# Turned rows of X: DRAM writes issued from another queue, and the last batch's staging tiles in another ring

## The chip, the cores and the metric

The kernel runs on one NeuronCore of a Trainium2 chip. The metric is the device time of one execution in microseconds (us). The core has five engines with instruction streams of their own: TensorE (PE in the profile), VectorE (DVE), ScalarE (ACT), GpSimd (POOL) and SyncE (SP). SP does nothing here but issue DMAs; GpSimd computes and can issue DMAs too. Each issuing engine has a DMA queue of its own, and all queues are served by the same 16 DMA engines.

## The reference, cut to what matters

Shapes: batch B = 4, sequence S = 448, model width DM = 768. Three stages follow one another:

```python
x = sigmoid_attention(q, k, v)                 # (4, 448, 768)
u = x + (x.T @ U @ V).T                        # mixing over tokens, low rank
x = u + relu(u @ w_ch1) @ w_ch2                # inner width 3072
theta = x @ w_theta
y = w_tok_r @ (x * cos(theta)) + w_tok_i @ (x * sin(theta))   # mixing over tokens
u = x + y
out = u + relu(u @ w_ch)
```

All is float32; each matrix product is done as three products of a high and a low part.

## The kernel before

X is kept on chip in one tile `X[128, 6, 1792]`: partitions and the index d (0 to 5) hold the 768 columns of the model, the last axis the 4 x 448 tokens. The order of instructions on each engine is the order in which the code issues them; nothing is reordered afterwards.

**The multilayer stage.** `i` runs over 12 slices of the inner width and `b` over the 4 batches. `ch1(i, b)` makes a slice (36 matmuls, L665 to L667), `ch2(i, b)` multiplies it back (three PSUM tiles `y`, numbered e2 = 0 to 2, two buffers; L687 to L689), and VectorE adds each `y` tile to X (L691). `ch2` runs one batch behind `ch1`. After each `y` tile a hook issues side work: steps of weight conversion on VectorE, ScalarE and GpSimd, and, in the last slice (`i == L`), the turns described now.

**The turns.** The last stage needs X with tokens on the partitions. VectorE turns each 128x448 piece of X in blocks of 32x32 (`turn_x`, L717) into a staging tile, and a DMA of 224 KB writes that tile to the DRAM array `x_d` (L718). There are 24 such pieces, six for each batch. Those of batches 0 to 2 are turned in the hooks of the last slice, two after each `y` tile, into the tile `stg` with three buffers: the fourth turn has to wait until the first turn's write has landed, and so on. Those of batch 3 come after the last `ch2`, into buffers of the tags `t1` and `t2` (two buffers each), so that the fifth turn there waits for the first one's write.

**The theta stage.** The 1792 tokens are taken in 14 chunks c of 128. `project(c, ...)` multiplies a chunk by w_theta (six weight rows `th_r`, kk = 0 to 5, L809 to L813) into one of two PSUM buffers `th`. `trig(c)` reads that buffer on VectorE (L845, L846) and makes sine and cosine on ScalarE. `load_xn(c)` reads a chunk of `x_d` with four DMAs (L822), `zmake(c)` multiplies, and `zsplit` splits the products into high and low parts in the rings `zh` and `zl` of 12 buffers each; the low parts are made on GpSimd (L112). `mix(b)` is the mixing over tokens (L909 to L914). The first two chunks are begun before the last two rows of w_theta have come: `project` is called for kk = 0 to 3 of chunks 0 and 1, then for kk = 4 and 5. Rows 4 and 5 of w_theta are loaded (`load_kept`, L236) from DRAM on SP's queue as soon as the last `ch2` has released their buffers. Behind them on SP's queue, in this order, stand the eight reads of `load_xn(0)` and `load_xn(1)`, and then the six writes of batch 3's turns.

Of the kernel before, what the change touches and what calls it, by code (L numbers as in the profile page):

```python
# [11 lines left out]
F32 = mybir.dt.float32  # L12
# [12 lines left out]
def tile_kernel(  # L25
# [15 lines left out]
    nc = tc.nc  # L41
    B, H, S, D = q.shape
# [3 lines left out]
    P = 128  # L46
# [8 lines left out]
    HN = DM // 2  # L55
# [44 lines left out]
    def pool(name, side="left", space=None):  # L100
        st = ExitStack()
        kw = dict(name=name, bufs=1, side=side, reuse_waits="tile")
        if space is not None:
            kw["space"] = space
        return st.enter_context(tc.tile_pool(**kw)), st
# [107 lines left out]
    x_d = dpool.tile([DM, NT], F32, name="x_d")  # L213
# [385 lines left out]
    for p in range(NP):  # L599
# [19 lines left out]
        b, r = divmod(p - 2 - NH, NH)  # L619
# [3 lines left out]
        b, r = divmod(p - 3 - NH, NH)  # L623
# [91 lines left out]
    ps_y, ps_y_st = pool("ps_y", "left", PSUM)  # L715
    def turn_x(b, d, t):
        nc.vector.transpose(out=t, in_=X[:, d, b * S:(b + 1) * S])  # L717
        nc.sync.dma_start(out=x_d[d * P:(d + 1) * P, b * S:(b + 1) * S], in_=t)  # L718

    def hook(i, b):  # L720
        def after(e2):
            if i == L and 0 < b < B:
                for d in (2 * e2, 2 * e2 + 1):
                    turn_x(b - 1, d, late["stg"].tile([P, S], F32, tag="stg", name=f"stg_{b}_{d}", bufs=3))
            if (i, b) == (0, 1):
                ps = ps_g.tile([P, FB, 512], F32, tag="g", name=f"hl_{e2}", bufs=2)
                U2(B - 1, 2 * e2, ps, (vhl, vll))
            if i == 0 and b in (1, 2):
                split_u(b + 1, u23, 2 * e2, 2 * e2 + 2, lo_pool)
            tick(i, b, e2 + 2)  # L730
        return after
# [63 lines left out]
    zp, st = pool("zp")  # L795
# [122 lines left out]
    load_xn(0)  # L918
    load_xn(1)
    for d in range(NK):  # L920
        tag = f"t{d % 2 + 1}"
        t = zp.tile([P, 2, HN], F32, tag=tag, name=f"stg_{B}_{d}", bufs=2).rearrange("p a n -> p (a n)")[:, :S]
        turn_x(B - 1, d, t)
    project(0, th_t, "th", 0, 4)
    project(1, th_t, "th", 0, 4)
# [108 lines left out]
```

## Time and profile before

| | us |
|---|---|
| median of three runs | 1178.91 (1177.11 to 1180.7) |
| the profiled execution, its own time | 1180.31 |
| its span, first to last instruction | 1178.5 |
| PE busy | 1153.6 (98%) |
| DVE busy | 667.1 (57%) |
| ACT busy | 360.3 (31%) |
| POOL busy | 190.9 (16%) |

The multilayer stage's last slice runs from about 820 to 883 us of the span, the theta stage from 883 to 1035. A busy share is an average over the whole span. PE stands still for 25 us in all, so what matters for the time is in which places those lie and what ends each.

### The profile page before, as it was taken

The page shows a single profiled execution, that of the slowest core. Times are in us where ns is not written, and L with a number is a line of the kernel's source. Part 1 is how long each engine was busy: PE and PEld are TensorE (multiplying, and loading weights), DVE is VectorE, ACT ScalarE, POOL GpSimd, SP SyncE. Part 2 cuts the span into 40 slices and gives each one's busy share as a digit, 9 for nine tenths or more (in the row PEclk, how much of TensorE's full clock was granted, in tenths as well). Part 3 has the DMA queues.
Part 4 walks back from the last instruction along what each step waited for, and adds up shares of the span by engine and source line. Part 5 has one row for each costly group of instructions (what it writes and reads, how often), then busy time and mean ns, then how long its engine had stood idle before and what let it go on. Part 6 is the DMA issues. An engine that isn't in the chain of part 4 may idle for free.

```text
span 1178.5 us, 15645 instructions
## 1 busy us (share of the span) xinstructions
PE 1153.6 (98%) x6336; PEld 995.9 (85%) x6336; DVE 667.1 (57%) x829; ACT 360.3 (31%) x465; POOL 190.9 (16%) x138
## 2 busy tenths in 40 slices
PE   7999999999999999999999999999998999999998
PEld 4354458999999999999999999999888899999997
DVE  4777873445555655556555656565485742833443
ACT  5878872221212121212121213131114431630110
POOL 2300012211211021102110212121001421320000
PEclk9999999999999999999999999999998999999999
DMA  9887730113231322132213333332557311230444
GB/s 163 157 175 134 159 83 1 55 54 96 71 111 54 96 84 98 54 96 85 96 54 97 96 107 107 107 108 107 210 204 177 55 22 20 44 145 1 57 65 67
DMA packets 227944, 111.20 MB, mean 94 GB/s; under 512 B 192384, under 2 KB 218880, under 8 KB 227744
## 3 DMA queue, kind: packets, MB, share of 16 engines
q1 hardware_dynamic: 201024, 98.57, 32.2%
q0 software_dynamic: 2368, 8.24, 2.6%
q10 hardware_dynamic: 24480, 3.39, 2.0%
q8 instruction: 50, 0.82, 0.3%
q14 instruction: 22, 0.18, 0.1%
HBM read 86.51 MB, written 23.66 MB: 93 GB/s over the span
## 4 chain that ended last, share of the span: by engine, by line
PE 87%; DVE 5%; DMA 4%; SPq 2%; issue 1%; ACT 1%; POOL 0%; ACTq 0%; DVEq 0%
PE g L665 10%; PE g L666 10%; PE g L667 10%; PE y L687 9%; PE y L689 9%; PE y L688 9%; PE av L420 4%; PE sc L394 3%; PE y L909 3%; PE y L910 3%; PE y L911 3%; PE wc L996 2%; PE wc L998 2%; PE wc L997 2%; DMA q<-in_q_dram 2%; PE th L813 1%
## 5 line engine op out<-in xcount | busy, mean ns | idle before, releaser
L691 DVE TENSOR_TENSOR X<-y,X 128x896 f32<-128x896 f32 x144 | 157.0, 1091 | 112.4 <-PE y L689 111.0
L687 PE MATMUL y<-gh,w 128*128 128x448 f32 x576 | 211.5, 367 | 4.8 <-DVE X L691 4.8
L689 PE MATMUL y<-gh,w 128*128 128x448 f32 x576 | 211.0, 366 | 0.0
L688 PE MATMUL y<-gl,w 128*128 128x448 f32 x576 | 210.9, 366 | 0.0
L665 PE MATMUL g<-uh,w 128*128 128x448 f32 x576 | 210.9, 366 | 0.0
L666 PE MATMUL g<-ul,w 128*128 128x448 f32 x576 | 210.5, 365 | 0.0
L667 PE MATMUL g<-uh,w 128*128 128x448 f32 x576 | 210.4, 365 | 0.0
L672 ACT ACTIVATE gh<-g 128x896 fp32r<-128x896 f32 x48 | 44.1, 919 | 393.0 <-PE g L667 393.0
L673 DVE SCALAR_TENSOR_TENSOR gl<-g,gh 128x896 fp32r<-128x896 f32 x48 | 52.4, 1092 | 174.8 <-ACT gh L672 174.8
L112 POOL TENSOR_TENSOR w<-ca_w,w 128x768 fp32r<-128x768 f32 x42 | 77.8, 1853 | 432.0 <-ACT w L109 432.0
L687 PEld LDWEIGHTS y<-gh,w 128*128 128x128 f32 x576 | 108.5, 188 | 15.8 <-DVE X L691 5.0
L665 PEld LDWEIGHTS g<-uh,w 128*128 128x128 f32 x576 | 108.3, 188 | 9.9 <-ACT uh L109 0.7
L689 PEld LDWEIGHTS y<-gh,w 128*128 128x128 f32 x576 | 108.5, 188 | 8.6
L688 PEld LDWEIGHTS y<-gl,w 128*128 128x128 f32 x576 | 108.5, 188 | 8.5
L667 PEld LDWEIGHTS g<-uh,w 128*128 128x128 f32 x576 | 108.3, 188 | 8.6
L666 PEld LDWEIGHTS g<-ul,w 128*128 128x128 f32 x576 | 108.3, 188 | 8.6
L385 ACT ACTIVATE A<-sc,bias_s 128x896 f32<-128x896 f32 x72 | 72.0, 1006 | 23.1 <-PE sc L394 13.3
L420 PE MATMUL av<-A,v 128*64 128x448 f32 x288 | 64.5, 556 | 0.0
L909 PE MATMUL y<-tok,zh 128*128 128x448 f32 x168 | 61.6, 367 | 1.4 <-DVE X L914 1.4
L809 PE MATMUL th<-th_r,xh 128*128 128x384 f32 x168 | 57.5, 342 | 4.8 <-DVE t L846 4.8
L112 POOL TENSOR_TENSOR zl<-t,zh 128x768 fp32r<-128x768 f32 x23 | 43.6, 1920 | 114.3 <-ACT zh L109 78.0
L911 PE MATMUL y<-tok,zl 128*128 128x448 f32 x168 | 61.5, 366 | 0.0
(142 smaller groups left out, 1645.7 us busy)
## 6 DMA issues: line engine op xcount, KB each, us to landing
ws_w<-in_moe_w_ch_dram SPq DMA_DIRECT2D x40, 768.0 KB, 4.4
ws_w<-in_moe_w_ch_dram POOLq DMA_DIRECT2D x8, 768.0 KB, 6.2
x_d<-stg SPq DMA_DIRECT2D x24, 224.0 KB, 2.0
k<-in_k_dram SPq DMA_DIRECT2D x94, 56.0 KB, 2.5
q<-in_q_dram SPq DMA_DIRECT2D x93, 56.0 KB, 3.4
xn<-x_d SPq DMA_DIRECT2D x52, 96.0 KB, 3.3
ws_th<-in_moe_w_theta_dram SPq DMA_DIRECT2D x6, 768.0 KB, 4.4
th_d<-sp_th SPq DMA_DIRECT2D x6, 768.0 KB, 4.0
```

The costliest lines, as they stand in the source:

```text
L112: nc.gpsimd.tensor_sub(o, a, b)
L385: nc.scalar.activation(a, ps, AF.Sigmoid, bias=bias_s, scale=SCALE)
L420: nc.tensor.matmul(ps[h * D:(h + 1) * D, :S], v_t[p // 2][:, 2 * (p % 2) + h, c, :], A_t[p, c][:, h, :], start=c == 0 and p % 2 == 0, stop ...
L665: nc.tensor.matmul(o, wh[:, sl], uh_t[b][:, kk, :], start=kk == 0, stop=False)
L666: nc.tensor.matmul(o, wh[:, sl], ul_t[b][:, kk, :], start=False, stop=False)
L667: nc.tensor.matmul(o, wl[:, sl], uh_t[b][:, kk, :], start=False, stop=kk == NK - 1)
L687: nc.tensor.matmul(o, wh[:, sl], gh[:, j, :], start=j == 0, stop=False)
L688: nc.tensor.matmul(o, wh[:, sl], gl[:, j, :], start=False, stop=False)
L689: nc.tensor.matmul(o, wl[:, sl], gh[:, j, :], start=False, stop=j == FB - 1)
L691: nc.vector.tensor_add(x, ps[:, :, :S], x)
L909: nc.tensor.matmul(o, zh[:, sl], tok_h[:, i, :], start=n == 0, stop=False)
L911: nc.tensor.matmul(o, zl[:, sl], tok_h[:, i, :], start=False, stop=n == NZ - 1)
```

## The change

All 24 writes of turned pieces are issued by GpSimd in place of SP. The six staging tiles of batch 3 come from the ring `zh` (12 buffers) in place of `t1` and `t2` (two each), so that each of the six has a buffer of its own.

```diff
@@ -715,7 +715,7 @@
     def turn_x(b, d, t):
         nc.vector.transpose(out=t, in_=X[:, d, b * S:(b + 1) * S])
-        nc.sync.dma_start(out=x_d[d * P:(d + 1) * P, b * S:(b + 1) * S], in_=t)
+        nc.gpsimd.dma_start(out=x_d[d * P:(d + 1) * P, b * S:(b + 1) * S], in_=t)
@@ -918,8 +918,7 @@
     load_xn(0)
     load_xn(1)
     for d in range(NK):
-        tag = f"t{d % 2 + 1}"
-        t = zp.tile([P, 2, HN], F32, tag=tag, name=f"stg_{B}_{d}", bufs=2).rearrange("p a n -> p (a n)")[:, :S]
+        t = zp.tile([P, 2, HN], F32, tag="zh", name=f"stg_{B}_{d}", bufs=12).rearrange("p a n -> p (a n)")[:, :S]
         turn_x(B - 1, d, t)
```

## Rows read from the trace of the kernel before

**Rows 1.** Windows: length, busy us of five engines, PEclk, DMA share, GB/s
```profile
834.00:848.00 14.00, 14.00 (x71) 12.97 (x70) 5.35 (x9) 0.92 (x1) 0.00 (x0) 1.00 0.92 365
848.00:856.00 8.00, 5.14 (x24) 4.08 (x23) 7.93 (x11) 2.51 (x3) 0.00 (x0) 0.98 0.24 86
856.00:859.00 3.00, 3.00 (x10) 2.69 (x9) 2.97 (x4) 0.00 (x0) 0.00 (x0) 0.50 0.45 158
859.00:884.00 25.00, 23.04 (x112) 20.42 (x111) 19.95 (x27) 4.04 (x5) 1.85 (x1) 1.00 0.60 224
884.00:896.00 12.00, 12.00 (x70) 11.74 (x68) 2.82 (x5) 0.85 (x1) 0.00 (x0) 1.00 1.01 248
896.00:901.00 5.00, 0.16 (x2) 0.13 (x1) 3.29 (x5) 0.18 (x1) 0.00 (x0) 0.91 0.86 291
901.00:907.00 6.00, 6.00 (x19) 6.00 (x20) 3.87 (x5) 5.89 (x7) 0.00 (x0) 0.51 0.37 57
...
934.00:1035.00 101.00, 100.56 (x542) 96.83 (x543) 53.05 (x61) 40.49 (x49) 28.42 (x17) 1.00 0.24 45
```

**Rows 2.** VectorE's timeline, first stall: start, us, operation, [idle before <- releaser]
```profile
835.65 1.17 DVE L717 STREAM_TRANSPOSE stg<-X 128x448 f32<-128x448 f32 x2
...
847.20 0.65 DVE L717 STREAM_TRANSPOSE stg<-X 128x448 f32<-128x448 f32 x1 [8.25 <-DMA x_d<-stg]
```

**Rows 3.** Tile view of x_d, the write issued at 836.3
```profile
DMA to landing us min/median/max: 10.8/10.8/10.8
```

**Rows 4.** TensorE's timeline, 849 to 855
```profile
849.74 0.47 PE L687 MATMUL y<-gh,w 128*128 128x448 f32 x1 [0.65 <-DVE X L691]
...
854.65 0.47 PE L687 MATMUL y<-gh,w 128*128 128x448 f32 x1 [2.21 <-DVE X L691]
```

**Rows 5.** VectorE's timeline, second stall
```profile
884.60 2.22 DVE L717 STREAM_TRANSPOSE stg<-X 128x448 f32<-128x448 f32 x4
...
897.67 1.19 DVE L717 STREAM_TRANSPOSE stg<-X 128x448 f32<-128x448 f32 x2 [10.85 <-DMA x_d<-stg]
898.80 0.96 DVE L845 TENSOR_SCALAR t<-th 128x768 f32<-128x768 f32 x1
```

**Rows 6.** SP's timeline, 884 to 900 (its own time)
```profile
884.69 9.78 SPq L822 DMA_DIRECT2D xn<-x_d  x8
894.57 4.65 SPq L718 DMA_DIRECT2D x_d<-stg  x6
```

**Rows 7.** Tile view of th_r, the last of the six loads
```profile
L236 SPq DMA_DIRECT2D th_r<-th_d x1: 858/858/858, 883.8 to 883.8; - x1
...
DMA to landing us min/median/max: 8.5/8.5/8.5
```

**Rows 8.** TensorE's timeline around the second stall and after
```profile
891.74 0.33 PE L809 MATMUL th<-th_r,xh 128*128 128x384 f32 x1
...
892.78 0.33 PE L809 MATMUL th<-th_r,xh 128*128 128x384 f32 x1
...
900.90 0.66 PE L809 MATMUL th<-th_r,xh 128*128 128x384 f32 x1 [4.84 <-DVE t L846]
...
933.84 0.47 PE L909 MATMUL y<-tok,zh 128*128 128x448 f32 x1 [1.39 <-DVE X L914]
```

**Rows 9.** Tile view of ws_U, eight loads issued from GpSimd
```profile
L271 POOL DMA_DIRECT2D ws_U<-in_moe_U_dram x8: 546/590/673, 30.5 to 34.5; - x8
...
DMA to landing us min/median/max: 2.2/3.9/6.0
```

**Rows 10.** Windows, as rows 1, during those loads
```profile
32.00:34.00 2.00, 2.00 (x16) 0.42 (x14) 1.93 (x5) 1.97 (x3) 2.00 (x5) 1.00 1.02 191
```

**Rows 11.** VectorE's timeline, last two turns of batch 2
```profile
877.79 1.17 DVE L717 STREAM_TRANSPOSE stg<-X 128x448 f32<-128x448 f32 x2
```

**Rows 12.** Tile view of x_d, the third and fourth writes of batch 2
```profile
L718 SPq DMA_DIRECT2D x_d<-stg x2: 320/320/320, 875.4 to 875.9; - x2
...
DMA to landing us min/median/max: 2.0/2.0/2.0
```

## The prediction

> **What bounds the kernel now.** I read windows over the stages around the turns first, for where PE stands still and at which clock, then the timelines of VectorE, PE and SP at the two places that the windows point to. PE is the bound nearly everywhere: from 934 to 1035 it is busy 100.56 of 101 us [rows 1], so whatever is gained or lost before 934 is carried to the end, and nothing later is touched by the change. The idle time that the change can reach lies at two places, and each begins with VectorE waiting for a write to `x_d`.
>
> First place. At 835.65 VectorE makes the first two turns of batch 0. The fourth must have the first one's buffer back. That write was issued at 836.3 and landed 10.8 us later [rows 3], so VectorE stood still for 8.25 us before 847.20 [rows 2]. The DMA engines were busy 0.92 of the time at 365 GB/s from 834 to 848 [rows 1], with loads that SP had issued ahead of the turns. The reader is to see the cost two steps on: PE needs `y` buffers that the late additions on VectorE release, and stands still for 0.65 us before 849.74 and 2.21 us before 854.65 [rows 4]. Then its granted clock is at 0.50, that is 1.2 GHz, from 856 to 859, and 0.98 as a mean in the 8 us before [rows 1]. That costs 3 x 0.5 + 8 x 0.02 = 1.7 us more. PE's other idle time here, 1.96 us from 859 to 884 [rows 1], falls where VectorE is busy for 19.95 of 25 us with other work; it stays.
>
> Second place. At 884.60 VectorE makes four turns of batch 3 and then waits 10.85 us, until 897.67, for the first write [rows 5]. SP could not issue that write before 894.57, since the eight reads of `x_d` ahead of it took SP from 884.69 to then [rows 6], with the DMA engines busy 1.01 from 884 to 896 [rows 1]. Behind the waiting turn on VectorE stand the last turn and `trig(0)`, which begins at 898.80 [rows 5]. PE, out of PSUM buffers, stands still for 4.84 us until 900.90 [rows 8] and then runs at a clock of 0.51 until 907 [rows 1]. After that PE isn't the bound for a while: at 933.84 it still waits 1.39 us for VectorE's addition [rows 8], so the chain of VectorE that starts with `trig(0)` sets the time there. What counts at this place is by how much `trig(0)` starts earlier; the slow clock from 901 to 907 is absorbed and I count it at nothing.
>
> **The change part by part.** *Removed from SP.* 24 issues of 0.32 us each [rows 12], on an engine that computes nothing: worth nothing by itself. What stood behind them on SP, reads of later chunks, goes out sooner; those aren't late now.
>
> *Added on GpSimd.* Each issue occupies the engine: 0.59 us is the median of eight loads that GpSimd issued around 30 us [rows 9], so 24 x 0.59 = 14 us on an engine that does no work of its own from 834 to 859 and 1.85 us of it from then to 884 [rows 1]. In program order a low part of a converted weight stands behind the last writes of batch 2, and the low parts of the theta stage behind those of batch 3; both are needed after these writes have long been issued. Zero, as long as VectorE's turns aren't late.
>
> *Landing time of a write from GpSimd's queue.* The trace has no write from there. The nearest rows are those eight loads of 16 and 96 KB: 2.2 us at least, 3.9 median, 6.0 at most [rows 9], with the DMA engines busy 1.02 and VectorE 1.93 of 2 us [rows 10]. A write on SP with the DMA engines free lands in 2.0 us [rows 12]. I take 3.9 us, since both places of interest are busy too; 2.0 and 6.0 are the bounds.
>
> *First place after.* The first write lands at 836.3 + 3.9 = 840.2 in place of 847.1, the fourth turn comes 7 us earlier, and so does the addition that PE lacked before 849.74 and 854.65. Gain: 0.65 + 2.21 + 1.7 = 4.5 us. Even at 6.0 us the turn would be 4.8 us earlier, enough for both gaps.
>
> *A new wait.* The three `stg` buffers remain. The tightest place is the sixth turn of a batch, which needs the third one's write: that was issued at 875.4 [rows 12], and the sixth turn begins half of 1.17 us after 877.79 [rows 11], at 878.4. The room is 3.0 us. SP's 2.0 us fits; 3.9 us is late by 0.9 us. Behind that turn on VectorE stand a conversion step and the addition for which the last `ch2` waits. In batches 0 and 1 VectorE has idle time to take it up; in batch 2 I count 0.9 us. Bounds: 0, and at 6.0 us a loss of 3.0. First place together: 4.5 - 0.9 = 3.6 us.
>
> *Second place after.* The six turns of batch 3 wait for nothing: VectorE is through with them some 3.5 us after 884.60. `trig(0)` then waits for PE to finish `project(0)`. In the profile PE began row kk = 4 of chunk 0 at 891.74 and kk = 5 at 892.78 [rows 8], 1.04 us each, so `project(0)` ends at about 893.9. At best `trig(0)` begins there, 898.8 - 893.9 = 4.9 us earlier. But the writes now go out while w_theta's row 5 is still coming. It was issued at 883.8 and landed 8.5 us later, at 892.3 [rows 7], 0.5 us before PE used it, with the DMA engines saturated. Six writes are 6 x 229,376 bytes = 1.38 MB; at 365/0.92 = 397 GB/s [rows 1] that is 3.5 us of all DMA engines. If most of it gets between, say 3.0 us, row 5 lands at 895.3, PE waits 2.5 us for it, `project(0)` ends at 896.4 and `trig(0)` begins at 896.5: 2.3 us gained. If all 3.5 us come first and that row runs at half clock, 0.8 us is gained; if none does, 4.9. I take 2.3, as the writes are all issued within 4 us and well before row 5 would be through. The reads of chunks 0 and 1 are delayed likewise, but their products come some 8 us behind `trig(0)`.
>
> *The rest.* `t1`, `t2` and `zh` keep their sizes; the z tiles that take over the six buffers come more than 10 us after those writes.
>
> **Sum.** 3.6 + 2.3 = 5.9 us. The profiled span becomes 1178.5 - 5.9 = 1172.6, its execution 1180.31 - 5.9 = 1174.4. The median of the runs shown is 1.4 us under that execution, so I predict 1178.91 - 5.9 = 1173.0 us.
>
> **The rivals.**
>
> *Row 5 isn't delayed* (its packets go first, or the writes are slow to start). Then 3.6 + 4.9 = 8.5 us: 1170.4. For it: the load is issued 1 us or more ahead of the first write. Against it: at 1.01 busy, what is put in has to push something out.
>
> *The queue makes no difference at the first place*: the writes still land in some 10 us from 834 to 848, because the same DMA engines are full. Then only the second place gains, 2.3 us: 1176.6. For it: 365 GB/s of loads is in the way whoever issues. Against it: loads from GpSimd landed in 3.9 us with the engines 1.02 busy; but SP's backlog at that moment was perhaps shorter. The Trainium skill, DMA: Bandwidth & Descriptors, section Issuing engines are not separate DMA queues, says that DMAs of all issuing engines run on the same 16 engines and that spreading them saves only issue time; by that rule alone it is this rival. The same page, section Queues, rings and completion order, has each DMA engine taking turns between the queues' rings by packet, which would let a short write pass a long backlog; no run here shows either for a write.
>
> *Slower: GpSimd can't prepare its transfers while VectorE is busy.* VectorE works almost without a gap where the turns stand. If each write then lands L us after issue, the sixth turn of each of three batches is late by L - 3.0. At L = 9 that is 6 us a batch. Batch 0's is less than the present stall of 8.25 us; the other two cost 12 us, of which the 5 us that VectorE idles between 859 and 884 [rows 1] take part. Net 7 lost there, 2.3 won later: 1178.9 + 4.7 = 1183.6. It decides from L of about 7 us. Against it: the eight loads took GpSimd 0.55 to 0.67 us each [rows 9], with VectorE busy 1.93 of 2 us [rows 10]. The Trainium skill, SBUF — State Buffer, section SBUF: two separate sides, says that GpSimd can't write its descriptors while a VectorE operation of a two-port mode runs, and that such a DMA seems blocked; by that rule the time goes towards this rival, and the early loads here don't show such a delay.
>
> *No gain*: another wait of VectorE's chain, such as ScalarE's or GpSimd's low parts, eats the second place, and the new wait the first. 1178 to 1179.
>
> **How the numbers follow.** Chances: forecast 0.48 (own range 1171 to 1175.4), row 5 undelayed 0.20, no difference at the first place 0.17, starved GpSimd 0.10, no gain 0.05. 0.3% of 1178.9 is 3.5 us, about what a measurement can tell. Faster by more, under 1175.4: 0.46 + 0.20 + 0.06 of the third (if row 5 isn't late there either) = 0.72. Within it: 0.02 + 0.11 + 0.05 = 0.18. Slower: 0.10. Range: at best 4.5 + 4.9 = 9.4 gives 1169.5, and a little for the measurement 1168.5; at the upper end it takes in the third case and stops at 1178, leaving out the slower one and part of the last.
>
> **What would show it.** VectorE's wait for a write at the fourth turn of batch 0 under 3 us, and none in batch 3; PE's gaps of 0.65 and 2.21 us gone, with no clock of 0.50 there; a wait of PE for `th_r` of about 2.5 us before kk = 5 of chunk 0; writes landing in 3 to 5 us. I'd be wrong if a write lands in over 7 us, if new waits for `x_d` stand at the sixth turns, or if PE's wait for `th_r` is over 4 us.

## The result, and the profile after

The changed kernel took 1168.4 us (median of five runs, 1167.84 to 1169.27), the kernel before 1178.48 us beside it: ratio 0.9915, 95% interval 0.9901 to 0.993. The gain is 10.1 us where 5.9 was forecast, and 1168.4 lies 0.1 us below the range. A second set of runs of the same kernel (the last experiment) gave 0.9933 (0.9919 to 0.9948), a gain of 8.5 us. The profiled execution shown here took 1167.84 us, with a span of 1166.1.

The first turn of batch 0 stands at 833.58 in this profile and at 835.65 in that of before [rows 2]. What lies ahead of it isn't touched by the change, so these 2.07 us are a difference of two executions, and I take them off below.

Windows of the changed kernel over the same stages as [rows 1], each about 2 us earlier at the first place, columns as there:

```profile
832.00:846.00 14.00, 14.00 (x71) 12.97 (x70) 8.60 (x13) 1.39 (x2) 3.11 (x6) 1.00 0.92 378
846.00:854.00 8.00, 8.00 (x40) 7.22 (x40) 7.90 (x11) 1.82 (x3) 1.44 (x3) 1.00 0.44 162
854.00:857.00 3.00, 3.00 (x17) 2.78 (x16) 2.96 (x5) 0.00 (x0) 1.07 (x2) 1.00 0.87 278
...
886.00:891.00 5.00, 4.82 (x26) 4.18 (x25) 3.27 (x4) 3.42 (x4) 0.00 (x0) 1.00 0.96 236
...
901.00:906.00 5.00, 3.16 (x17) 2.55 (x16) 4.97 (x4) 2.63 (x3) 3.54 (x2) 0.99 0.00 0
906.00:909.00 3.00, 3.00 (x11) 3.00 (x10) 2.97 (x5) 2.43 (x3) 1.81 (x2) 0.50 0.02 5
```

In the second line PE is busy 8.00 of 8 us where it was 5.14, and in the third the granted clock is 1.00 where it was 0.50. Behind the turns of batch 3, where TensorE had 0.16 us of work in 5 us before, the line from 886 to 891 shows 4.82. A stretch at 0.50 (1.2 GHz) is left at 906, behind a stretch in which PE was busy 3.16 of 5 us (901 to 906).

VectorE's timeline of the changed kernel, the lines that answer to [rows 2, 5, 11], with two more that the explanation needs:

```profile
833.58 1.17 DVE L717 STREAM_TRANSPOSE stg<-X 128x448 f32<-128x448 f32 x2
...
841.84 0.65 DVE L717 STREAM_TRANSPOSE stg<-X 128x448 f32<-128x448 f32 x1 [4.96 <-DMA x_d<-stg]
...
870.88 1.30 DVE L717 STREAM_TRANSPOSE stg<-X 128x448 f32<-128x448 f32 x2
...
877.87 3.27 DVE L717 STREAM_TRANSPOSE stg<-X 128x448 f32<-128x448 f32 x6
...
887.70 0.96 DVE L845 TENSOR_SCALAR t<-th 128x768 f32<-128x768 f32 x1 [6.55 <-PE th L813]
...
893.14 0.96 DVE L118 TENSOR_TENSOR xl<-X,xh 128x768 fp32r<-128x768 f32 x1 [0.77 <-ACT xh L109]
```

The fourth turn still waits, but 4.96 us instead of 8.25. The six turns of batch 3 run as one piece. `trig(0)` (L845) now waits for TensorE, not for a turn. The last line is the low part of X for a later chunk; before, VectorE's timeline had it so:

```profile
905.57 0.96 DVE L118 TENSOR_TENSOR xl<-X,xh 128x768 fp32r<-128x768 f32 x1 [2.10 <-ACT xh L109]
```

With three marks the whole difference can be read off, each as a distance between two instructions, so that the 2.07 us drop out:

| stretch on VectorE | before | after | gained |
|---|---|---|---|
| first turn of batch 0 to first turn of batch 3 | 48.95 | 44.29 | 4.66 |
| from there to `trig(0)` | 14.20 | 9.83 | 4.37 |
| from there to that `xl` | 6.77 | 5.44 | 1.33 |
| from there to the end of the span | 272.93 | 272.96 | 0 |

The sum is 10.36 us; the spans differ by 1178.5 - 1166.1 - 2.07 = 10.33. The first two terms are the two places of the forecast (3.6 and 2.3 us there), the third it didn't have.

Some 1.2 to 1.6 us of the first term belong to this one execution of the kernel before. Three kernels below keep the writes of batches 0 to 2 on SP and so have the same stall: the ring alone, batch 3 from GpSimd, and the early sine. Their first stretch is 47.40, 47.70 and 47.42 us. TensorE's two gaps are there (0.48 to 0.76 and 2.21 to 2.22 us), but its granted clock stays at 1.00 behind them, where [rows 1] have 0.50 for 3 us. The kernel with the early sine, its windows and VectorE's timeline:

```profile
847.00:855.00 8.00, 5.12 (x25) 4.09 (x23) 7.93 (x11) 2.51 (x3) 0.00 (x0) 1.00 0.24 86
855.00:858.00 3.00, 3.00 (x16) 2.79 (x15) 2.97 (x4) 0.00 (x0) 0.00 (x0) 1.00 0.45 158
```
```profile
834.67 1.17 DVE L717 STREAM_TRANSPOSE stg<-X 128x448 f32<-128x448 f32 x2
...
882.09 2.21 DVE L717 STREAM_TRANSPOSE stg<-X 128x448 f32<-128x448 f32 x4
```

The kernels that write batches 0 to 2 from GpSimd take 43.99 to 44.46 us for this stretch. Beside the three executions without the slow clock the first place thus gains 2.9 to 3.7 us. In how many executions of the kernel before the clock falls there isn't known. The second term varies as well: the second profile of the changed kernel has 10.31 us in place of 9.83, a gain of 3.89.

The landing times, from the tile views of the changed kernel: the first write of batch 0 (issued at 834.5), and the third and fourth writes of batch 2, which answer to [rows 3, 12]:

```profile
L718 POOL DMA_DIRECT2D x_d<-stg x1: 790/790/790, 834.5 to 834.5; - x1
...
DMA to landing us min/median/max: 7.3/7.3/7.3
```
```profile
L718 POOL DMA_DIRECT2D x_d<-stg x2: 540/540/540, 871.8 to 872.5; - x2
...
DMA to landing us min/median/max: 2.2/2.3/2.3
```

Among the loads a write from GpSimd lands in 7.3 us, where SP's took 10.8; for the later writes of batch 2 it is 2.2 to 2.3, where SP's took 2.0. The last load of w_theta's row 5, answering to [rows 7]:

```profile
L236 SPq DMA_DIRECT2D th_r<-th_d x1: 849/849/849, 876.9 to 876.9; - x1
...
DMA to landing us min/median/max: 9.4/9.4/9.4
```

It is 0.9 us slower than the 8.5 of before, not 3.0. TensorE began kk = 4 at 884.99 and kk = 5 at 886.33, which is 0.3 us more than the 1.04 us that a row takes. In the second profile of this kernel row 5 landed in 9.9 us and kk = 5 began 0.8 us late.

### The profile page after: what moved, and what is told of

Same layout as the page of the kernel before. It is cut to its first block, busy times and chain, and to the rows that moved or that the text cites. A ratio compares the mean times of both kernels' runs of the same rounds, so it can differ in the third digit from the quotient of the medians.

```text
span 1166.1 us, 15652 instructions
## 1 busy us (share of the span) xinstructions
PE 1149.5 (99%) x6336; PEld 993.5 (85%) x6336; DVE 667.5 (57%) x829; ACT 360.1 (31%) x465; POOL 204.2 (18%) x162
## 4 chain that ended last, share of the span: by engine, by line
PE 90%; DVE 3%; SPq 3%; DMA 2%; issue 1%; ACT 0%; POOL 0%; ACTq 0%; DVEq 0%
PE g L665 10%; PE g L667 10%; PE g L666 10%; PE y L687 10%; PE y L689 10%; PE y L688 10%; PE av L420 4%; PE sc L394 3%; PE y L909 3%; PE y L910 3%; PE y L911 3%; PE wc L995 2%; PE wc L996 2%; PE wc L997 2%; PE th L813 2%; SPq L319 1%
## 5 line engine op out<-in xcount | busy, mean ns | idle before, releaser
L909 PE MATMUL y<-tok,zh 128*128 128x448 f32 x168 | 61.6, 367 | 0.0
L910 PE MATMUL y<-tok,zh 128*128 128x448 f32 x168 | 61.5, 366 | 0.0
```

Source lines behind the costliest of these rows:

```text
L909: nc.tensor.matmul(o, zh[:, sl], tok_h[:, i, :], start=n == 0, stop=False)
L910: nc.tensor.matmul(o, zh[:, sl], tok_l[:, i, :], start=False, stop=False)
```

## The experiments

The diffs are against the changed kernel, but for the fifth. Each group ran beside the kernel before on one chip.

### One part at a time: four kernels

**The ring alone.** All writes on SP as before, batch 3 in the ring `zh`.

```diff
-        nc.gpsimd.dma_start(out=x_d[d * P:(d + 1) * P, b * S:(b + 1) * S], in_=t)
+        nc.sync.dma_start(out=x_d[d * P:(d + 1) * P, b * S:(b + 1) * S], in_=t)
```

> All 24 writes on SP's queue as before; only batch 3's staging tiles move to the ring of 12. Theory A (three separate gains: 4.5 us at the first place from GpSimd's queue, 4.4 us at the second place from six turns that need no buffer back, 1.3 us because ScalarE's table load no longer waits for a staging write): the first place stays, the other two gains remain, 5.7 us under the kernel before, about 1172.8; VectorE's wait of 8.25 us at the fourth turn of batch 0 stays, trig(0) starts when project(0) ends. Rival B (the queue is what counts at both places, since on SP a write stands behind eight reads): no gain over 1 us, 1178.

1172.78 us, ratio 0.9951 (0.9939 to 0.9963). VectorE's timeline of this kernel:

```profile
846.59 0.65 DVE L717 STREAM_TRANSPOSE stg<-X 128x448 f32<-128x448 f32 x1 [8.08 <-DMA x_d<-stg]
...
882.62 3.27 DVE L717 STREAM_TRANSPOSE stg<-X 128x448 f32<-128x448 f32 x6
...
892.04 0.96 DVE L845 TENSOR_SCALAR t<-th 128x768 f32<-128x768 f32 x1 [6.15 <-PE th L813]
```

The first stall is that of before. At the second place `trig(0)` comes 9.42 us after the first turn instead of 14.20: 4.78 us gained, which is the forecast's "best" of 4.9. Row 5 landed in 8.5 us. So the six turns' wait was nearly the whole obstacle there.

**GpSimd's queue for batches 0 to 2 alone.** Batch 3 writes from SP, out of `t1` and `t2`, as before.

```diff
+        (nc.sync if b == B - 1 else nc.gpsimd).dma_start(...)
...
-        t = zp.tile(..., tag="zh", ..., bufs=12)...
+        tag = f"t{d % 2 + 1}"
+        t = zp.tile(..., tag=tag, ..., bufs=2)...
```

> The writes of batches 0 to 2 on GpSimd's queue, batch 3's writes and staging tiles as before. Theory A: only the first place gains, 4.5 us: about 1174.0; the wait of 10.9 us at the fifth turn of batch 3 and the table load's wait stay. Rival C (the first place's gain is swallowed later, since VectorE's chain after 885 waits for a DMA that doesn't come earlier): under 2 us, 1177 or more.

1174.41 us, 0.9959 (0.9947 to 0.9971). The first wait is 4.83 us, the second 10.63, as before. The queue gains 4.8 us (0.0041 x 1179; 3.4 to 6.2 by the interval) at the first place by itself. With the ring's 5.8 us (0.0049 x 1179) it makes 10.6; the two add up to what the change gains within the intervals.

**Batch 3 from GpSimd, the others from SP.**

```diff
+        (nc.gpsimd if b == B - 1 else nc.sync).dma_start(...)
```

> The writes of batches 0 to 2 on SP as before; batch 3 as in the changed kernel (GpSimd's queue and the ring of 12). Theory A: 4.4 + 1.3 = 5.7 us under the kernel before, 1172.8, and the same as with SP's queue for batch 3, since a write that nobody waits for may be issued anywhere. Rival D (the writes on GpSimd's queue hold up the last row of w_theta by some 3 us, as I had forecast, and in the changed kernel something else made up for it): 2 to 3 us slower than the ring alone with SP's queue, 1175 to 1176.

1174.0 us, 0.9953 (0.994 to 0.9966), between the two expected times; the ratio can't be told from that of the ring alone. Row 5 landed in 9.8 us and TensorE's waits list

```profile
PE th L809 <- DMA th_r<-th_d: 0.6, 1, 0.6
```

`trig(0)` came 10.32 us after the first turn, 0.9 later than with the ring alone. So the mechanism of the forecast, the writes delaying row 5, exists, with a wait of 0.6 us where 2.5 was forecast.

**All writes from GpSimd, no ring.** Only the tags `t1` and `t2` of before are put back.

> All 24 writes on GpSimd's queue, batch 3's staging tiles in the two tags of two buffers as before. Theory A: the first place gains 4.5 us; at the second the fifth turn waits for the first write, which lands some 7.4 us after its issue, about when project(0) ends, so most of the 4.4 us is gained, but the table load waits for the fourth turn's write again, so 0 to 1.3 of the 1.3 us: 1169 to 1171. Rival E (the ring of 12 is what counts at the second place): only 4.5 us, 1174.

1171.94 us, 0.9935 (0.9923 to 0.9947), a little above what was expected. VectorE still stands for 6.53 us before the fifth turn, nearly all of it inside its wait for TensorE, since `trig(0)` waits 0.25 us more:

```profile
888.57 1.26 DVE L717 STREAM_TRANSPOSE stg<-X 128x448 f32<-128x448 f32 x2 [6.53 <-DMA x_d<-stg]
890.09 0.96 DVE L845 TENSOR_SCALAR t<-th 128x768 f32<-128x768 f32 x1 [0.25 <-PE th L813]
```

That places `trig(0)` at 10.26 us after the first turn, and the `xl` behind it at 6.78 us after that, as before the change. Together 1.8 us of the 3.5 us that this kernel is behind the changed one. Of the rest, its profile has 1.27 us behind the `xl` (274.23 us to the end of the span instead of 272.96). TensorE's granted clock there is 0.69 as a mean from 911 to 918, behind 7 us in which TensorE was busy 3.86; in the changed kernel the mean from 908 to 915 is 0.90, behind 7 us with 5.16 busy. That this slower clock makes the 1.27 us isn't tested. The 6.78 belongs to the third term.

### The third term: ScalarE's table load

ScalarE must load its table for sine once in the theta stage. Its timeline before and after, around that load:

```profile
893.67 0.85 ACT L109 ACTIVATE xh<-X 128x768 fp32r<-128x768 f32 x1 [12.80 <-PE th L810]
900.82 1.28 ACT L847 ACT_TABLE_LOAD   x1 [6.30 <-DVE t L846]
902.12 0.84 ACT L847 ACTIVATE t<-t 128x768 f32<-128x768 f32 x1
```
```profile
887.33 0.85 ACT L109 ACTIVATE xh<-X 128x768 fp32r<-128x768 f32 x1 [13.38 <-PE th L810]
888.20 1.28 ACT L847 ACT_TABLE_LOAD   x1
889.68 0.85 ACT L847 ACTIVATE t<-t 128x768 f32<-128x768 f32 x1 [0.20 <-DVE t L846]
```

Before, the load starts only when VectorE has made the operand of the sine (L846); after, it runs beside VectorE's work. A load needs no operand, so the reason must be in the program. The compiled one, before and after (the number is the instruction's place on its engine):

```
before  354 L847 ACT_TABLE_LOAD [waits DMAHW1_49,DVE_49]
        355 L847 ACTIVATE ...   [waits Pool_49]
after   354 L847 ACT_TABLE_LOAD
        355 L847 ACTIVATE ...   [waits DVE_49]
```

The sine's tile was a staging tile in the kernel before, so it had several things to wait for, one of them a write to `x_d`, and some of these waits stand in front of the load. With the staging tiles in another ring one wait is left, and it stands on the sine itself. The test is the kernel before with a sine of one column that nothing uses, ahead of the theta stage, so that the table is there early:

```diff
     ch2(*prev, hook(NB - 1, B))
+    nc.scalar.activation(warm, half_pi, AF.Sin)
     th_t[4] = load_kept("th4", "w2")
```

> The kernel before with one sine of a single column added on ScalarE after the last product of the multilayer stage, so that the sine table is loaded while ScalarE is idle. Theory A (in the kernel before, the table load of 1.28 us stood on the path because it had inherited the wait for a staging write and for VectorE; in the changed kernel it runs under VectorE's subtraction): about 1.3 us under the kernel before, VectorE's wait for xh of 2.1 us down to 0.8. Rival F (the 1.3 us come from the earlier start of VectorE's chain): no gain, wait for xh still 2.1 us.

1177.8 us beside 1179.1, ratio 0.9989 (0.998 to 0.9998): 1.3 us by the medians, 0.2 to 2.4 by the interval, in line with the third term. The load stands at 878.36 now, and VectorE's wait for `xh` in its waits list is near that of the changed kernel (0.77), not of before (2.10):

```profile
DVE xl L118 <- ACT xh L109: 0.8, 1, 0.8
```

The Trainium skill, ScalarE: Activation LUTs, section What ACT_TABLE_LOAD costs, gives about 1283 ns for a load, which is the 1.28 us here, and a drain of about 1380 ns besides; no such drain shows, as the sine at 902.12 follows the load's end at 902.10, and in the changed kernel the load at 888.20 follows the conversion's end at 888.18.

### The first place: is a wait of 4.96 us still paid for?

**A fourth staging buffer.** `stg` with four buffers in place of three.

```diff
-  ... late["stg"].tile([P, S], F32, tag="stg", name=f"stg_{b}_{d}", bufs=3)
+  ... late["stg"].tile([P, S], F32, tag="stg", name=f"stg_{b}_{d}", bufs=4)
```

> The changed kernel with four buffers of stg in place of three. VectorE's wait of 5.0 us at the fourth turn of batch 0 goes, or moves to the fifth and shrinks by some 3 us. Theory A (that wait is covered: the addition behind it is early enough for TensorE anyway): no gain, within 0.5 us of the changed kernel, 1168.4. Rival G (the wait still costs TensorE time through the additions that follow): 1 to 3 us faster, 1165.5 to 1167.5.

1169.29 us, 0.992 (0.9907 to 0.9933), the changed kernel's time. VectorE's waits list for writes here, and in the changed kernel:

```profile
DVE stg L717 <- DMA x_d<-stg: 3.0, 2, 2.2
```
```profile
DVE stg L717 <- DMA x_d<-stg: 5.0, 1, 5.0
```

Two microseconds of that wait are gone and nothing is gained, so at least these lay under TensorE's own work, which the changed kernel's windows show without a gap from 832 to 854. The profile is that of the slowest of the six executions, 1173.54 us; its excess lies ahead of the turns, the first of which stands at 839.43, and the stretch from there to the first turn of batch 3 takes 44.00 us.

**ScalarE's queue.** All writes issued by ScalarE.

```diff
-        nc.gpsimd.dma_start(out=x_d[...], in_=t)
+        nc.scalar.dma_start(out=x_d[...], in_=t)
```

> The changed kernel with all writes on ScalarE's queue in place of GpSimd's. Theory A (what matters is a queue other than the one with the loads): the writes land at the first place in about 7 us too, against 7.3 from GpSimd and 10.8 from SP, and in 2 us elsewhere; ScalarE waits behind late turns, which costs at most 2 us: 1168 to 1171. Rival H (writes from GpSimd are served in some other way): they land in 10 us again and the first place's gain is lost: 1173.

1176.01 us, 0.9974 (0.9964 to 0.9983), slower than I expected. The first write landed in 8.4 us, so this queue, too, passes SP's backlog in part, but ScalarE's timeline shows another price:

```profile
835.75 12.51 ACTq L718 DMA_DIRECT2D x_d<-stg  x6
848.36 0.92 ACT L672 ACTIVATE gh<-g 128x896 fp32r<-128x896 f32 x1 [15.07 <-DVE stg L717]
```

Six issues take 12.51 us, as each waits until VectorE has turned its piece, and the conversion of `gh` that TensorE needs stands behind them. TensorE's waits for VectorE's additions sum to 6.1 us; in the changed kernel they are 2.1. Its granted clock was 0.69 as a mean from 870 to 880, behind such waits, where the changed kernel has 1.00. GpSimd was a good place since nothing urgent stands behind a waiting write there.

### The second place: who pays for the six writes?

**Batch 3 from SP, batches 0 to 2 from GpSimd.** Here SP's order puts the six writes behind the reads of chunks 0 and 1, so they can't get between row 5 and its landing.

```diff
+        (nc.sync if b == B - 1 else nc.gpsimd).dma_start(...)
```

> GpSimd's queue for batches 0 to 2, SP's queue and the ring of 12 for batch 3. Theory A: the last row of w_theta lands 8.5 us after issue in place of 9.4, so trig(0) starts 0.3 to 0.9 us earlier than in the changed kernel: 1167.5 to 1168.4. Rival I (batch 3 behind the reads on SP makes a later wait for x_d): 1169 or more.

1168.48 us, 0.9909 (0.9897 to 0.9922); row 5 landed in 8.4 us, and `trig(0)` came 9.39 us after the first turn, 0.4 to 0.9 sooner than in the two profiles of the changed kernel. The time is the changed kernel's within the intervals, so which queue carries batch 3 matters by less than these can tell once the ring is there.

**Twice the bytes.** Batch 3's writes carry each staging tile twice (448 KB, into a wider `x_d`; the second copy is never read).

```diff
+        if b == B - 1:
+            nc.gpsimd.dma_start(
+                out=x_d[d * P:(d + 1) * P, b * S:(b + 2) * S].rearrange("p (a s) -> p a s", a=2),
+                in_=t.unsqueeze(1).to_broadcast([P, 2, S]))
+            return
```

> The changed kernel, but each of batch 3's six writes from GpSimd carries its tile twice (448 KB, into a wider x_d whose last part nobody reads), so 2.75 MB in place of 1.38 stand beside the last load of w_theta. Theory S (while GpSimd's queue has work it gets a share of the DMA engines, whatever is behind; what it takes beyond that comes from the reads of x_d that stand behind the load on SP's queue): the load of row 5 lands 9.4 to 10 us after issue, as in the changed kernel, and the reads of chunk 0 land later, near 14 us in place of 11.6; the time is within 1 us of the changed kernel. Theory V (each byte written delays the load by as much, as my forecast had it): the load lands 0.9 to 3.5 us later than in the changed kernel, and TensorE waits for it by 1.4 to 4 us.

**Half the bytes.** Of each piece of batch 3 GpSimd writes half the columns, SP the other half behind its reads.

```diff
+        if b == B - 1:
+            h = b * S + S // 2
+            nc.gpsimd.dma_start(out=x_d[d * P:(d + 1) * P, b * S:h], in_=t[:, :S // 2])
+            nc.sync.dma_start(out=x_d[d * P:(d + 1) * P, h:(b + 1) * S], in_=t[:, S // 2:])
+            return
```

> The changed kernel, but of each of batch 3's six tiles half the columns are written from GpSimd's queue and half from SP's, behind the reads. Theory S: the load of row 5 lands 8.5 to 9.4 us after issue; theory V with the forecast's size: 10.

1170.25 us, 0.9929 (0.9917 to 0.9942), for twice the bytes; 1168.66 us, one run, for half. Landing times from the tile views of `th_r` (its last load) and `xn` (the first read of chunk 0, next behind it on SP's queue):

| written from GpSimd beside row 5 | row 5, us | first read, us |
|---|---|---|
| nothing (ring alone; batch 3 from SP; the cosine kernel below) | 8.5, 8.4, 8.9 | 8.2, 8.0, 8.2 |
| 0.69 MB (half) | 9.4 | 10.2 |
| 1.38 MB (the changed kernel, and again; batch 3 from GpSimd; four `stg`) | 9.4, 9.9, 9.8, 9.5 | 11.6, 12.0, 12.1, 11.7 |
| 2.75 MB (twice) | 10.1 | 15.8 |

The rows behind two of these entries, the first read of `xn` in the changed kernel and the reads at that place with twice the bytes:

```profile
L822 SPq DMA_DIRECT2D xn<-x_d x1: 319/319/319, 877.9 to 877.9; - x1
...
DMA to landing us min/median/max: 11.6/11.6/11.6
```
```profile
L828 SPq DMA_DIRECT2D xn<-x_d x2: 319/569/819, 878.9 to 879.2; - x2
...
DMA to landing us min/median/max: 15.6/15.7/15.8
```

The first column grows by 0.5 to 1.0 us at the first 0.69 MB and by little after, hardly more than it differs between profiles at one dose. The second grows by 3.4 to 4.1 us from none to 1.38 MB and by 3.7 to 4.2 from there to 2.75 MB: about the 3.5 us of all DMA engines that the forecast worked out for 1.38 MB. At twice the bytes the slack of these reads is used up: VectorE waits for them, 0.24 and 1.28 us, as it doesn't in the changed kernel.

**A cosine part on VectorE.** The kernel of batch 3 from SP, with chunk 0's low part of the cosine product made on VectorE instead of GpSimd, since VectorE waits 1.7 us for GpSimd in this stage.

```diff
-            zsplit((b, i), cos, lo_pool)
+            zsplit((b, i), cos, lo_dve if c == 0 else lo_pool)
```

> Batches 0 to 2 on GpSimd's queue, batch 3 on SP's with the ring of 12, and the low part of chunk 0's first product made on VectorE in place of GpSimd, whose wait of 1.7 us holds up trig(2). If VectorE's chain is what sets the time between 885 and 920, as theory A has it, 0 to 1.5 us under 1168.4; if TensorE's waits there are covered otherwise, no change.

1169.36 us, 0.9921 (0.9908 to 0.9934), not to be told from 1168.48. The wait for GpSimd is gone, but VectorE waits 2.3 us for ScalarE's `zh` instead, and TensorE has new waits at the mixing.

**The changed kernel again**, beside those of the last group.

> The changed kernel once more beside the three others, as their reference: 1168.4 within 1 us.

1169.79 us (six runs, 1168.6 to 1173.54) beside 1178.31, 0.9933 (0.9919 to 0.9948). No kernel here beats the changed one by more than the intervals.

## Why the prediction missed

Its direction and its two places were right; the size was not. Of the 4.46 us between 5.9 and the 10.36 of the table above, the second place holds 2.07, the term that was missing 1.33 and the first place 1.06. By its own steps:

**First place: near in sum, with terms that were off.** Forecast 4.5 less 0.9, measured 4.66 beside the profile that the forecast was made from, and 2.9 to 3.7 beside the three executions in which the clock didn't fall. The two gaps were priced rightly. The 1.7 us for the clock hold for an execution like the profiled one, and the forecast took that one for all. A write was to land in 3.9 us; it took 7.3, as the nearest rows had been 16 and 96 KB loads, not a write of 224 KB. The forecast's own mark for being wrong was "over 7 us", and VectorE's wait of 4.96 us misses its sign of "under 3 us". It didn't matter: the fourth turn came 8.26 us after the first instead of 11.55, and these 3.3 us cover both gaps of TensorE (0.65 and 2.21), and no slow clock follows. Of the rest of VectorE's wait at least 2 us are covered, as the fourth buffer shows.

**A new wait: it didn't come.** I charged 0.9 us for sixth turns that would wait for a write of 3.9 us. From GpSimd such writes landed in 2.2 to 2.3 us, inside the room of 3.0; the two last turns of batch 2 run back to back but for some 0.1 us (1.30 us at 870.88 instead of 1.17). I had taken a landing time from rows with the DMA engines 1.02 busy for a stretch where they were 0.60 busy [rows 1].

**Second place: the term that failed.** I let "most of" the six writes' 3.5 us get between row 5 and its landing: row 5 late by 3.0, TensorE waiting 2.5, gain 2.3. Row 5 was late by 0.9 (1.4 in the second profile), TensorE by 0.3 (0.8), and the gain was 4.37 (3.89), of 4.78 with no write beside it. The volume was priced rightly and charged to the wrong transfer. Row 5's load had been issued 1.9 us before the first write (876.9 to 878.8) and most of its bytes seem to have gone ahead; what stood behind it on SP's queue, the reads of chunk 0, took the 3.5 us, and by the forecast's own reading those are wanted some 8 us after `trig(0)`. The dose of bytes shows this. How exactly the 16 engines share their time between the two queues is not shown, only when transfers land.

**What was missing.** That "the chain of VectorE that starts with `trig(0)`" sets the time was right, but I followed it by one link only. The wait of 2.10 us for `xh`, behind ScalarE's table load, was in VectorE's timeline of before. It holds 1.33 us: the stretch from `trig(0)` to the `xl` is 5.44 to 5.49 us in every kernel with the ring or the early sine and 6.77 to 6.78 in those with neither. The line of the waits there named VectorE's operand, though, and that the change would free the load could only be read from the compiled program.

**The rivals.** "Row 5 isn't delayed" (8.5 us) was nearest; with the new wait at nothing and the third term it is 4.66 + 4.78 + 1.33 = 10.8, or 9.0 to 9.8 beside an execution in which the clock doesn't fall. "The queue makes no difference at the first place" is refuted by batches 0 to 2 alone, 4.8 us faster. The rule of the Trainium skill (DMA: Bandwidth & Descriptors, section Issuing engines are not separate DMA queues) that spreading saves only issue time therefore doesn't hold for a short write behind a long backlog: 10.8 us on SP, 8.4 on ScalarE, 7.3 on GpSimd, 3.5 us less than on SP, where an issue takes SP 0.32 us. GpSimd was not starved, either. Its timeline of the changed kernel has six issues while VectorE turns without a gap from 877.87 to 881.14:

```profile
878.80 3.22 POOL L718 DMA_DIRECT2D x_d<-stg  x6 [2.88 <-DVE stg L717]
```

0.54 us each, less than the 0.59 forecast. "No gain" fell with the result.

## What to carry to other kernels

When bytes are added beside a saturated stretch, price them by volume, and then ask which transfer stands at the back of the queue: that one pays, and it may have slack. Follow the chain behind a freed stall at least to the next engine that it waits for, since a second stall a few instructions on, here ScalarE's table load, may go with it. A write that must pass a backlog of loads belongs on the queue of an engine on which nothing urgent stands behind it.

## What the runs showed that I had not expected

- **An SP queue that holds itself up.** In the compiled program each DMA that SP issues waits for the one eight places before it, by one of eight counters that are used in turn, beside its own data:

```
338 L822 DMA xn_7008<-x_d      [waits DMAHW6_49]
346 L718 DMA x_d<-stg_0_7018   [waits DMAHW6_49,DVE_49]
```

  So in the kernel before the eight reads could be issued only as earlier loads landed (9.78 us for eight issues [rows 6]), and batch 3's first write behind them. In the changed kernel one read's issue took 6.8 us. GpSimd's DMAs have eight counters of their own, with nothing long on them in this stretch. That this is the reason for the long issues is argued from program and trace; no run took the counters away.
- **A table load that waits for data.** ScalarE's load of 1.28 us stood behind a DMA and a VectorE operation that only the sine needed.
- **A slow clock in some executions only.** Behind the same two gaps of TensorE the granted clock was 0.50 for 3 us in one of four profiled executions and 1.00 in three.
- **Three queues, three landing times** for the same write beside the same loads: 10.8, 8.4 and 7.3 us (10.7 to 11.0 in four profiles from SP, 6.8 to 7.4 in nine from GpSimd, one from ScalarE). What sets the order of the last two is open.
